# Two score rounds and two AV rounds at a time, gate steps spread over later pairs, and x rows stored unnormalised per pair

## The chip, the cores and the metric

The kernel runs on one core of a Trainium2 chip. The metric is the device time of one execution in microseconds (us). Instruction times come from one profiled execution; in its rows PE is TensorE's matmul side, PEld its weight loads, DVE is VectorE, ACT is ScalarE, POOL is GpSimd and SP the engine that issues most of the DMAs.

## The reference, cut to what matters

An attention with normalised q and k feeds a mixture of experts. The attention output, laid out as N = 3584 rows of 768 values, is the experts' input x; each row goes to the one expert with the highest logit, and each expert keeps at most 80 rows, those with the largest gate weight.

```python
# B, H, S, D = 8, 12, 448, 64;  E, F, capacity = 8, 1024, 80
q_n, k_n = rmsnorm(q, g_q), rmsnorm(k, g_k)
scores = scale * np.matmul(q_n, k_n.transpose(0, 1, 3, 2))
attn = np.exp(scores - np.max(scores, axis=-1, keepdims=True))
attn = attn / (np.sum(attn, axis=-1, keepdims=True) + 1e-09)
x = np.matmul(attn, v).transpose(0, 2, 1, 3).reshape(B * S, H * D)
logits = x @ w_gate
expert_idx = np.argmax(logits, axis=1)
gate_w = softmax(logits)[np.arange(N), expert_idx]
for e in range(E):
    tok_idx = the 80 (or fewer) rows of expert e with the largest gate_w
    h = np.maximum(x[tok_idx] @ w1[e], 0.0)
    out[tok_idx] = gate_w[tok_idx, None] * (h @ w2[e])     # all other rows stay 0
```

## The kernel before, in words

**Attention.** The 96 heads are worked off as 48 pairs; the loop variable is n, and six pairs make one batch b. A pair's 448 keys are cut into four groups of 112, j = 0 to 3. For each j, `score` makes two matmuls (one head on array rows 0 to 63, the other on 64 to 127) into one of two PSUM buffers `ps` of two banks each, and ACT takes the exponential into `at` (buffers for two pairs). `av` then makes two matmuls per j (one head on array columns 0 to 63, the other on 64 to 127) that add up in `po`. There is one `po` buffer: `uevac` copies it to SBUF (`us`) on DVE, and only then can the next pair's first `av` start. The softmax is left unnormalised; `presum` adds the four groups of `at` on DVE into `sm`, and `zl` turns the sums and `us` of two pairs into row sums and gate logits by narrow matmuls.

**Preparing q and k.** `load_qk` runs four pairs ahead into three buffers. `square` (ACT) and `rstd` (a DVE reduction into `ssq`, then `ms` and `rs` on POOL) run three pairs ahead, `normalise` (two DVE multiplications into `qn`) two ahead, and `transp` (PE transposes into a `tp` buffer of PSUM, copied out by ACT) one ahead. The two `tp` buffers are shared with the transposes of the gate and of x.

**Gate and x.** After a batch, `gate1` and `gate2` make the logits' normalisation, the maximum, the gate weight and the masked scores (DVE with one exponential on ACT and transposes on PE) and write them to `S_sb`. `xout` transposes `us` back, DVE multiplies by the reciprocal row sums `rz` into a bf16 row buffer `xb`, and one DMA per batch stores it to a DRAM scratch. `us` has 12 buffers for this.

**Order.** Inside the attention the order of every engine is that of the code (a manual schedule). Engines run their own instructions in that order, so an instruction that waits holds up all that stand behind it on its engine. SP issues loads, zero stores to `out` and the x stores in one queue in the same way.

**Top 80 and experts.** Ten rounds of maximum, index and replacement over `S_sb` (8 x 3584) run on DVE alone. Expert weights (24 KB per partition for w1 and w2 of one expert) are fetched by POOL's DMA queue: experts 0 and 1 during the attention, at n = 2, 5, 8 and 11 (`NW0 = 2`); the others have five slots in the space that the attention leaves, so ten transfers are queued when it is over, and expert 7 waits for a slot. Behind them on the same queue stand the gathers of the experts' rows (`xg`), which PE transposes (`pxt`) for the two matmul stages `ph` and `py`.

Of the kernel before, what the change touches and what calls it, by code (L numbers as in the profile page):

```python
# [19 lines left out]
def kernel(  # L20
# [31 lines left out]
    xbf_dram = nc.dram_tensor("xbf_scratch", (N, DM), BF16, kind="Internal").ap()  # L52
# [38 lines left out]
    NW0 = 2  # L91
# [20 lines left out]
    with tc.tile_pool(name="qk", bufs=3) as qkpool, \  # L112
# [3 lines left out]
         tc.tile_pool(name="us", bufs=12) as upool, \  # L116
# [118 lines left out]
        def gate1(b):  # L235
            zsb = gpool.tile([128, S], F32, tag="zsb", name="zsb", bufs=1)
            nc.vector.tensor_copy(zsb[:, :], gst[b]["zl"][:, :S])
            zt = tpps.tile([128, 512], F32, tag="tp", name="zt")
            for j in range(NT):
                nc.tensor.transpose(zt[:ST, j * 128:(j + 1) * 128],  # L240
                                    zsb[:, j * ST:(j + 1) * ST], ident[:, :])
            ztv = zt[:ST, :].rearrange("p (j c r) -> p j r c", j=NT, c=4)
# [11 lines left out]
            gst[b]["xb"] = gpool.tile([ST, NT, DM], BF16, tag="xb", name="xb")  # L254

        def gate2(b):
# [16 lines left out]
            nc.vector.tensor_mul(sc[:], eq[:], gw[:].unsqueeze(2).to_broadcast([ST, NT, E]))  # L273
            sp = tpps.tile([128, 512], F32, tag="tp", name="sp")
# [26 lines left out]
        for n in range(-4, NP + 6):  # L301
# [11 lines left out]
            m = n - 3  # L313
            if ok(n):
                score(n, 0)
            if ok(n - 2):
                uevac(n - 2)
            if ok(n - 1):
                av(n - 1, 0)
                presum(n - 1)  # L320
            if ok(n + 1):
                transp(n + 1, 0)
            if ok(n):
                score(n, 1)
            if ok(n - 1):
                av(n - 1, 1)
            if ok(n - 2) and (n - 2) % 2 == 1:
                zl(n - 2)
            if ok(n + 2):
                normalise(n + 2)  # L330
            if ok(n):
                score(n, 2)
            if ok(n - 1):
                av(n - 1, 2)
            if ok(n + 1):
                transp(n + 1, 1)
            if ok(n):
                score(n, 3)
            if ok(n + 3):
                square(n + 3)  # L340
                rstd(n + 3)
            if ok(n - 1):
                av(n - 1, 3)
# [32 lines left out]
    with tc.tile_pool(name="moe_w2", bufs=1) as wlate, \  # L376
# [6 lines left out]
        for e in range(E):  # L383
# [6 lines left out]
            xg = mpool.tile([CAP, DM], BF16, tag="xg", name="xg")  # L390
            nc.vector.memset(xg[:, :], 0.0)
            nc.gpsimd.indirect_dma_start(
                out=xg[:, :], out_offset=None, in_=xbf_dram[:, :],
                in_offset=bass.IndirectOffsetOnAxis(ap=idx_e[:, :1], axis=0),
                bounds_check=N - 1, oob_is_err=False)
            pxt = mps.tile([128, DC, CAP], BF16, tag="pxt", name="pxt")
# [69 lines left out]
```

## Time and profile before

| | us |
|---|---|
| median of 3 runs | 963.59 (961.34 to 969.52) |
| the profiled execution, its own time | 962.24 |
| its span, first to last instruction | 960.3 |
| PE busy in the span | 594.2 (62%) |
| DVE busy | 488.1 (51%) |
| ACT busy | 287.2 (30%) |
| POOL busy | 180.9 (19%) |

The span has four stages, one after the other: the attention, the top-80 rounds on DVE alone, a stretch in which only weight transfers run, and the experts. A busy share over the whole span therefore says little; each stage is read for itself. The granted clock stands beside the stages: 1.00 is 2.4 GHz and 0.50 is 1.2 GHz.

### The profile page before, as it was taken

How to read it: one execution, taken by the hardware profiler on the slowest of the kernel's cores; microseconds unless marked ns; L12 is line 12 of the kernel's file. 1: busy time of each engine (PE TensorE's matmuls, PEld its weight loads, DVE VectorE, ACT ScalarE, POOL GpSimd, SP SyncE). 2: the span in 40 equal slices, each digit the busy share in tenths (PEclk: the TensorE clock that was granted, in tenths of full speed). 3: DMA queues.
4: the chain of work that ended last, by engine and by line, in shares of the span. 5: the costliest groups of instructions: out<-in, count | busy, mean ns of one | idle time of the engine just before them, and what ended most of it. 6: DMA issues, size and time to landing. Idle time of an engine off the chain costs nothing.

```text
span 960.3 us, 7959 instructions
## 1 busy us (share of the span) xinstructions
PE 594.2 (62%) x3120; PEld 220.9 (23%) x3120; DVE 488.1 (51%) x589; ACT 287.2 (30%) x361; POOL 180.9 (19%) x134
## 2 busy tenths in 40 slices
PE   1888788868878887788888879879600000000746
PEld 0322222223222322322232223223200000000634
DVE  2655546545545544644644554564699997000212
ACT  2544433433443444344344334434000000000101
POOL 2422212221221221212221221220000001200212
PEclk9999988988898898799798888979855555555879
DMA  3456252521321222132023213101100001999371
GB/s 97 127 136 140 80 131 63 135 75 45 103 75 53 69 85 74 45 103 75 29 63 115 75 45 103 55 26 46 48 30 0 0 0 19 202 211 211 71 147 52
DMA packets 57893, 78.20 MB, mean 81 GB/s; under 512 B 6145, under 2 KB 46593, under 8 KB 57857
## 3 DMA queue, kind: packets, MB, share of 16 engines
q1 hardware_dynamic: 42368, 49.59, 17.2%
q0 software_dynamic: 15488, 28.12, 15.8%
q8 instruction: 24, 0.39, 0.2%
q14 instruction: 13, 0.10, 0.0%
HBM read 84.38 MB, written 18.49 MB: 107 GB/s over the span
## 4 chain that ended last, share of the span: by engine, by line
PE 48%; another core or an unknown queue 21%; DVE 11%; issue 7%; DMA 6%; ACT 4%; SPq 1%; POOL 1%; POOLq 0%; ACTq 0%; DVEq 0%
PE ps L189 18%; PE po L199 15%; PE tp L174 5%; DVE ssq L151 4%; ACT sq L145 4%; DMA out_dram<-yo,idx_e 3%; PE xp L285 3%; DMA vt<-in_v_dram 3%; PE zl L228 2%; PE zl L232 2%; DVE us L216 1%; DVE qn L165 1%; PE ph L409 1%; DVE S_sb L277 1%
## 5 line engine op out<-in xcount | busy, mean ns | idle before, releaser
L199 PE MATMUL po<-at,vt 112*64 112x448 f32 x768 | 205.8, 618 | 64.8 <-DVE us L216 35.0
L193 ACT ACTIVATE at<-ps 112x896 f32<-112x896 f32 x192 | 176.1, 917 | 231.8 <-PE ps L189 231.8
L189 PE MATMUL ps<-qkT 64*112 64x448 f32 x768 | 224.4, 666 | 0.6 <-ACT qkT L181 0.6
L151 DVE TENSOR_REDUCE ssq<-sq 112x16 f32<-112x1024 f32 x48 | 58.5, 1220 | 278.7 <-ACT sq L145 278.7
L157 POOL TENSOR_TENSOR rs<-ms,nhalf 112x16 f32<-112x16 f32 x48 | 140.1, 2918 | 4.0
L398 PE MATMUL pxt<-identb,xg 80*128 80x80 bf16 x48 | 3.5, 224 | 211.0 <-DMA xg<-xbf_scratch,idx_e 211.0
L154 POOL TENSOR_SCALAR ms<-ssq 112x16 f32<-112x16 f32 x48 | 10.6, 220 | 483.1 <-DVE ssq L151 483.1
L199 PEld LDWEIGHTS po<-at,vt 112*64 112x64 f32 x768 | 41.9, 146 | 216.8 <-issue 144.8
L413 ACT ACTIVATE h_sb<-ph 128x320 bf16<-128x320 f32 x16 | 7.0, 438 | 258.3 <-PE ph L409 258.3
L174 PE MATMUL tp<-ident,qn 112*128 112x112 f32 x384 | 65.8, 301 | 20.8 <-DVE qn L165 20.8
L189 PEld LDWEIGHTS ps<-qkT 64*112 64x112 f32 x768 | 59.4, 192 | 77.8 <-issue 48.0
L165 DVE TENSOR_TENSOR qn<-qk,rs 112x512 f32<-112x512 f32 x96 | 61.8, 685 | 11.7 <-POOL rs L157 11.7
L174 PEld LDWEIGHTS tp<-ident,qn 112*128 112x128 f32 x384 | 43.1, 156 | 97.3 <-issue 77.4
L179 ACT ACTIVATE qkT<-tp,gqk 128x448 f32<-128x448 f32 x48 | 30.5, 635 | 111.7 <-PE tp L174 111.7
L211 DVE TENSOR_TENSOR sm<-t,t 112x896 f32<-112x896 f32 x48 | 52.4, 1092 | 1.7
L209 DVE TENSOR_TENSOR t<-at 112x896 f32<-112x896 f32 x48 | 52.2, 1087 | 0.0
L210 DVE TENSOR_TENSOR t<-at 112x896 f32<-112x896 f32 x48 | 51.9, 1082 | 0.0
L398 PEld LDWEIGHTS <-xg 80*128 80x128 bf16 x48 | 2.8, 112 | 212.1 <-issue 197.9
L145 ACT ACTIVATE sq<-qk 112x1024 f32<-112x1024 f32 x48 | 50.4, 1049 | 1.3 <-DVE ssq L151 1.3
L401 DVE COPY xgT<-pxt 128x480 bf16<-128x480 bf16 x8 | 3.1, 393 | 92.3 <-PE pxt L398 92.3
L102 POOL DMA_DIRECT2D w_sb<-in_moe_w_dram x8 | 7.2, 897 | 175.2 <-DMA gw_scratch<-gw_all 168.9
L289 DVE TENSOR_TENSOR xb<-xp,rz 112x512 bf16<-112x512 f32 x48 | 31.7, 686 | 16.8 <-PE xp L285 16.5
(56 smaller groups left out, 458.7 us busy)
## 6 DMA issues: line engine op xcount, KB each, us to landing
w_sb<-in_moe_w_dram POOLq DMA_DIRECT2D x16, 1536.0 KB, 25.0
qk<-in_q_dram SPq DMA_DIRECT2D x48, 224.0 KB, 3.0
qk<-in_k_dram SPq DMA_DIRECT2D x48, 224.0 KB, 3.5
vt<-in_v_dram SPq DMA_DIRECT2D x48, 224.0 KB, 3.9
out_dram<-zeros SPq DMA_DIRECT2D x28, 384.0 KB, 4.5
xbf_scratch<-xb SPq DMA_DIRECT2D x8, 672.0 KB, 4.7
idx_e<-idx_scratch SPq DMA_DIRECT2D x8, 0.3 KB, 2.1
gw_e<-gw_scratch SPq DMA_DIRECT2D x8, 0.3 KB, 5.7
```

The source lines that it names most:

```text
L145: nc.scalar.activation(sq[:, :], st[n]["qk"][:].rearrange("p a h x -> p (a h x)"), AF.Square)
L151: nc.vector.reduce_sum(out=ssq[:, :], in_=st[n]["sq"][:].rearrange("p (g d) -> p g d", d=D), axis=AX.X)
L157: nc.gpsimd.tensor_tensor(rs[:].rearrange("p a h j -> p (a h j)"), ms[:, :], nhalf[:, :], op=ALU.pow)
L165: nc.vector.tensor_mul(qn[:, a].rearrange("p j h d -> p h j d"), qk[:, a].rearrange("p h (j d) -> p h j d", d=D), rs[:, a].unsqueeze(3).to ...
L174: nc.tensor.transpose(tp[:, j * ST:(j + 1) * ST], st[n]["qn"][:, a, j].rearrange("p h d -> p (h d)"), ident[:ST, :ST])
L189: nc.tensor.matmul(ps[:, hh, :S], st[n]["T1"][hh * D:(hh + 1) * D, j * ST:(j + 1) * ST], st[n]["T0"][hh * D:(hh + 1) * D, :], start=True, ...
L193: nc.scalar.activation(st[n]["at"][:, j], ps[:, :, :S], AF.Exp)
L199: nc.tensor.matmul(st[n]["po"][hh * D:(hh + 1) * D, :S], st[n]["v"][:, hh, j * D:(j + 1) * D], st[n]["at"][:, j, hh, :], start=(j == 0), s ...
L209: nc.vector.tensor_add(t0[:], at[:, 0], at[:, 1])
L210: nc.vector.tensor_add(t1[:], at[:, 2], at[:, 3])
L211: nc.vector.tensor_add(sm[:], t0[:], t1[:])
L289: nc.vector.tensor_mul(xb[:, :, hp * 128:(hp + 1) * 128].rearrange("p j (h d) -> p j h d", d=D), xp[:ST, :].rearrange("p (j h d) -> p j h ...
```

## The change

In the attention's loop body, the four score rounds and the four AV rounds of a pair are issued as two and two. The copy of `po` moves from the next pair's second step to the end of its own pair's AV rounds. `square` moves ahead of the transposes, `rstd` behind the last two score rounds. The gate of a batch is split into `gate1`, `gate1t`, `gate1v`, `gate2` and `gate3`, spread over three pairs. `xout` runs for one pair in every step, two pairs behind; its PSUM result is copied by ACT as f32 without the multiplication, and one DMA per pair stores it into a scratch whose rows hold 768 values and 12 reciprocal row sums; these are stored by one small DMA per batch. The experts gather such rows as f32 and multiply by the reciprocals on DVE into `xn`. `us` has 4 buffers instead of 12, three experts' weights are fetched during the attention instead of two, and the late slots are four instead of five; `xg`, `xgT` and `h_sb` have two buffers instead of three.

```diff
-    xbf_dram = nc.dram_tensor("xbf_scratch", (N, DM), BF16, kind="Internal").ap()
+    XW = DM + H
+    xr_dram = nc.dram_tensor("xr_scratch", (N, XW), F32, kind="Internal").ap()
...
-    NW0 = 2
+    NW0 = 3
...
-        slot = e if e < NW0 else NW0 + (e - NW0) % 5
+        slot = e if e < NW0 else NW0 + (e - NW0) % 4
...
-         tc.tile_pool(name="us", bufs=12) as upool, \
+         tc.tile_pool(name="us", bufs=4) as upool, \
...
+            nc.sync.dma_start(
+                out=xr_dram[b * S:(b + 1) * S, DM:XW].rearrange("(p j) h -> p j h", j=NT),
+                in_=rz[:].rearrange("p j i c -> p j (i c)"))
...
-            xb, rz = gst[b]["xb"], gst[b]["rz"]
-            r = rz[:].rearrange("p j i c -> p j (i c)")[:, :, 2 * hp:2 * hp + 2]
-            nc.vector.tensor_mul(
-                xb[:, :, hp * 128:(hp + 1) * 128].rearrange("p j (h d) -> p j h d", d=D),
-                xp[:ST, :].rearrange("p (j h d) -> p j h d", j=NT, d=D),
-                r.unsqueeze(3).to_broadcast([ST, NT, 2, D]))
-            if hp == HP - 1:
-                nc.sync.dma_start(
-                    out=xbf_dram[b * S:(b + 1) * S].rearrange("(p j) d -> p (j d)", j=NT),
-                    in_=xb[:].rearrange("p j d -> p (j d)"))
+            xb = prep.tile([ST, NT, 128], F32, tag="xb", name="xb")
+            nc.scalar.copy(xb[:].rearrange("p j d -> p (j d)"), xp[:ST, :])
+            nc.sync.dma_start(
+                out=xr_dram[b * S:(b + 1) * S, hp * 128:(hp + 1) * 128].rearrange(
+                    "(p j) d -> p j d", j=NT),
+                in_=xb[:])
...
             if ok(n):
                 score(n, 0)
-            if ok(n - 2):
-                uevac(n - 2)
+                score(n, 1)
+            for b in range(B):
+                last = b * HP + HP - 1
+                if n == last + 3:
+                    gate1(b)
+                if n == last + 4:
+                    gate1v(b)
             if ok(n - 1):
                 av(n - 1, 0)
+                av(n - 1, 1)
                 presum(n - 1)
+            if ok(n + 3):
+                square(n + 3)
             if ok(n + 1):
                 transp(n + 1, 0)
+                transp(n + 1, 1)
+            if ok(n + 2):
+                normalise(n + 2)
+            for b in range(B):
+                if n == b * HP + HP - 1 + 4:
+                    gate2(b)
             if ok(n):
-                score(n, 1)
+                score(n, 2)
+                score(n, 3)
+            if ok(n + 3):
+                rstd(n + 3)
             if ok(n - 1):
-                av(n - 1, 1)
+                av(n - 1, 2)
+                av(n - 1, 3)
+                uevac(n - 1)
+            if ok(n - 2):
+                xout(n - 2)
             if ok(n - 2) and (n - 2) % 2 == 1:
                 zl(n - 2)
...
             for b in range(B):
                 last = b * HP + HP - 1
-                if n == last + 2:
-                    gate1(b)
                 if n == last + 3:
-                    gate2(b)
-                if last + 3 <= n < last + 6:
-                    xout(b * HP + 2 * (n - last - 3))
-                    xout(b * HP + 2 * (n - last - 3) + 1)
+                    gate1t(b)
+                if n == last + 5:
+                    gate3(b)
...
-            xg = mpool.tile([CAP, DM], BF16, tag="xg", name="xg")
+            xg = mpool.tile([CAP, XW], F32, tag="xg", name="xg", bufs=2)
...
+            xn = mpool.tile([CAP, DM], BF16, tag="xn", name="xn", bufs=2)
+            nc.vector.tensor_mul(
+                xn[:].rearrange("p (h d) -> p h d", d=D),
+                xg[:, :DM].rearrange("p (h d) -> p h d", d=D),
+                xg[:, DM:XW].unsqueeze(2).to_broadcast([CAP, H, D]))
```

PE, one pair in the first batch, before: `ps` is a score round, `po` an AV round of the pair before it, `tp` the transposes for the pair after it; numbers behind a name are buffers as the program counts them.

```order
L189 MATMUL ps_584<-qkT_531,qkT_561 112x448 x2
L199 MATMUL po_590<-at_510,vt_369 64x448 x2
L174 MATMUL tp_599<-ident_58,qn_547 128x112 x4
L189 MATMUL ps_606<-qkT_531,qkT_561 112x448 x2
L199 MATMUL po_590<-at_510,vt_369 64x448 x2
L189 MATMUL ps_615<-qkT_531,qkT_561 112x448 x2
L199 MATMUL po_590<-at_510,vt_369 64x448 x2
L174 MATMUL tp_621<-ident_58,qn_547 128x112 x4
```

PE, one pair in the first batch, after; `xp` is the transpose of x, two pairs behind.

```order
L191 MATMUL ps_692<-qkT_646,qkT_653 112x448 x2
L191 MATMUL ps_696<-qkT_646,qkT_653 112x448 x2
L201 MATMUL po_700<-at_619,vt_462 64x448 x4
L176 MATMUL tp_713<-ident_58,qn_655 128x112 x4
L176 MATMUL tp_720<-ident_58,qn_655 128x112 x4
L191 MATMUL ps_730<-qkT_646,qkT_653 112x448 x2
L191 MATMUL ps_734<-qkT_646,qkT_653 112x448 x2
L201 MATMUL po_700<-at_619,vt_462 64x448 x4
L301 MATMUL xp_750<-ident_58,us_676 112x128 x4
```

Score and AV rounds that alternated one by one now stand in twos, both transposes stand together, and each pair has one group of `xp`.

ACT, one pair, before (`qkT` are the copies of the transposes, `sq` the square).

```order
L193 ACTIVATE at<-ps 112x896
L179 ACTIVATE qkT<-tp,gqk 128x448
L193 ACTIVATE at<-ps 112x896 x2
L181 COPY qkT<-tp 128x448
L193 ACTIVATE at<-ps 112x896
L145 ACTIVATE sq<-qk 112x1024
```

ACT, one pair, after.

```order
L195 ACTIVATE at_691<-ps_692 112x896
L195 ACTIVATE at_691<-ps_696 112x896
L147 ACTIVATE sq_711<-qk_613 112x1024
L181 ACTIVATE qkT_718<-tp_713,gqk_70 128x448
L183 COPY qkT_725<-tp_720 128x448
L195 ACTIVATE at_691<-ps_730 112x896
L195 ACTIVATE at_691<-ps_734 112x896
L304 COPY xb_755<-xp_750 112x512
```

The square now has the copies of the transposes and two exponentials behind it, and the copy of x has come onto ACT.

POOL's DMA queue behind the attention, from the last late weight transfers to the gathers, before: ten transfers (five experts, the last two of them shown) stand ahead of the first gather `xg`.

```order
L102 DMA w1_sb_4088<-in_moe_w1_dram 128x6x1024
L106 DMA w2_sb_4089<-in_moe_w2_dram 128x8x768
L102 DMA w1_sb_4092<-in_moe_w1_dram 128x6x1024
L106 DMA w2_sb_4093<-in_moe_w2_dram 128x8x768
L392 DMA xg_4104<-xbf_scratch,idx_e_4100 80x768
```

The same queue, after: all eight.

```order
L104 DMA w1_sb_4168<-in_moe_w1_dram 128x6x1024
L108 DMA w2_sb_4169<-in_moe_w2_dram 128x8x768
L104 DMA w1_sb_4172<-in_moe_w1_dram 128x6x1024
L108 DMA w2_sb_4173<-in_moe_w2_dram 128x8x768
L104 DMA w1_sb_4176<-in_moe_w1_dram 128x6x1024
L108 DMA w2_sb_4177<-in_moe_w2_dram 128x8x768
L104 DMA w1_sb_4180<-in_moe_w1_dram 128x6x1024
L108 DMA w2_sb_4181<-in_moe_w2_dram 128x8x768
L406 DMA xg_4192<-xr_scratch,idx_e_4188 80x780
```

Two transfers fewer stand ahead of the first gather.

## Rows read from the trace of the kernel before

**Rows 1.** Stretches: busy PE, PEld, DVE, ACT, POOL; then PEclk, DMA share, GB/s.

```profile
26.00:690.00 664.00, 542.58 (x2527) 181.66 (x2528) 347.81 (x485) 273.77 (x338) 148.07 (x96) 0.88 0.29 80
...
710.00:830.00 120.00, 0.00 (x0) 0.00 (x0) 99.71 (x48) 0.00 (x0) 7.71 (x9) 0.50 0.16 26
```

**Rows 2.** Timeline of PE, two pairs: start, length, instructions, idle time before and releaser.

```profile
42.02 0.97 PE L199 MATMUL po<-at,vt 112*64 112x448 f32 x4 [1.91 <-DVE us L216]
...
43.55 1.84 PE L189 MATMUL ps<-qkT 64*112 64x448 f32 x4
45.31 1.65 PE L199 MATMUL po<-at,vt 112*64 112x448 f32 x4
...
54.02 0.97 PE L199 MATMUL po<-at,vt 112*64 112x448 f32 x4 [1.91 <-DVE us L216]
54.93 0.60 PE L174 MATMUL tp<-ident,qn 112*128 112x112 f32 x4
55.46 1.01 PE L189 MATMUL ps<-qkT 64*112 64x448 f32 x4
56.40 0.97 PE L199 MATMUL po<-at,vt 112*64 112x448 f32 x4
57.30 0.96 PE L228 MATMUL zl<-sm,zsel 112*32 112x448 f32 x8
...
58.94 1.01 PE L189 MATMUL ps<-qkT 64*112 64x448 f32 x4
```

**Rows 3.** Timeline of DVE at the end of the second pair.

```profile
64.27 1.22 DVE L151 TENSOR_REDUCE ssq<-sq 112x16 f32<-112x1024 f32 x1 [5.95 <-ACT sq L145]
65.41 0.61 DVE L216 COPY us<-po 128x448 f32<-128x448 f32 x1
```

**Rows 4.** Busy time in two short stretches of the same two pairs.

```profile
43.50:46.80 3.30, 3.30 (x9) 0.74 (x8) 2.77 (x4) 1.55 (x2) 2.25 (x2) 0.51 0.55 159
...
54.00:64.00 10.00, 9.98 (x56) 3.09 (x56) 4.28 (x5) 4.63 (x6) 2.74 (x1) 1.00 0.65 185
```

**Rows 5.** Timeline of PE at the last pair, where four AV rounds stand together.

```profile
677.60 3.23 PE L199 MATMUL po<-at,vt 112*64 112x448 f32 x16 [0.73 <-DVE us L216]
680.75 0.96 PE L228 MATMUL zl<-sm,zsel 112*32 112x448 f32 x8
```

**Rows 6.** Groups by line and shape: busy us, mean ns, idle before and releaser.

```profile
L193 ACT ACTIVATE at<-ps 112x896 f32<-112x896 f32 x192 | 176.1, 917 | 231.8 <-PE ps L189 231.8
L157 POOL TENSOR_TENSOR rs<-ms,nhalf 112x16 f32<-112x16 f32 x48 | 140.1, 2918 | 4.0
L165 DVE TENSOR_TENSOR qn<-qk,rs 112x512 f32<-112x512 f32 x96 | 61.8, 685 | 11.7 <-POOL rs L157 11.7
L209 DVE TENSOR_TENSOR t<-at 112x896 f32<-112x896 f32 x48 | 52.2, 1087 | 0.0
L145 ACT ACTIVATE sq<-qk 112x1024 f32<-112x1024 f32 x48 | 50.4, 1049 | 1.3 <-DVE ssq L151 1.3
L289 DVE TENSOR_TENSOR xb<-xp,rz 112x512 bf16<-112x512 f32 x48 | 31.7, 686 | 16.8 <-PE xp L285 16.5
L179 ACT ACTIVATE qkT<-tp,gqk 128x448 f32<-128x448 f32 x48 | 30.5, 635 | 111.7 <-PE tp L174 111.7
```

**Rows 7.** Timeline of DVE from the last gate scores to the first top-80 round.

```profile
688.39 0.94 DVE L277 COPY S_sb<-sp 8x448 f32<-8x448 f32 x1 [1.00 <-PE sp L276]
...
694.25 3.87 DVE L362 MAX8 gw_all<-S_sb 8x8 f32<-8x3584 f32 x1
```

**Rows 8.** Timeline of POOL and PE: first late transfer, third gather's issue, first expert's transposes.

```profile
811.61 0.89 POOL L102 DMA_DIRECT2D w_sb<-in_moe_w_dram  x1 [168.89 <-DMA gw_scratch<-gw_all]
...
853.99 0.96 POOL L392 DMA_INDIRECT xg<-xbf_scratch,idx_e  x1 [6.42 <-issue]
...
891.31 0.96 PE L398 MATMUL pxt<-identb,xg 80*128 80x80 bf16 x12 [197.70 <-DMA xg<-xbf_scratch,idx_e]
```

**Rows 9.** The loads of q and k, issue to landing over all 96.

```profile
DMA to landing us min/median/max: 2.4/3.3/9.4
```

More of the change, by code (lines that the diff above doesn't have):

```diff
@@ L237, in gate1, with gate1t @@
             nc.vector.tensor_copy(zsb[:, :], gst[b]["zl"][:, :S])
+            gst[b]["zsb"] = zsb
+        def gate1t(b):
+            zsb = gst[b]["zsb"]
             zt = tpps.tile([128, 512], F32, tag="tp", name="zt")
@@ L241, in gate1, with gate1v @@
                                     zsb[:, j * ST:(j + 1) * ST], ident[:, :])
+            gst[b]["zt"] = zt
+        def gate1v(b):
+            zt = gst[b]["zt"]
             ztv = zt[:ST, :].rearrange("p (j c r) -> p j r c", j=NT, c=4)
@@ L273, in gate2, with gate3 @@
             nc.vector.tensor_mul(sc[:], eq[:], gw[:].unsqueeze(2).to_broadcast([ST, NT, E]))
+            gst[b]["sc"] = sc
+        def gate3(b):
+            sc = gst[b]["sc"]
             sp = tpps.tile([128, 512], F32, tag="tp", name="sp")
@@ L312 @@
                 fetch_w2(n // 6)
-            m = n - 3
             if ok(n):
                 score(n, 0)
-            if ok(n - 2):
-                uevac(n - 2)
+                score(n, 1)
[5 more added lines that the diff above has]
+                    gate1v(b)
             if ok(n - 1):
                 av(n - 1, 0)
+                av(n - 1, 1)
                 presum(n - 1)
+            if ok(n + 3):
+                square(n + 3)
             if ok(n + 1):
                 transp(n + 1, 0)
+                transp(n + 1, 1)
[4 more added lines that the diff above has]
+                    gate2(b)
             if ok(n):
-                score(n, 1)
+                score(n, 2)
+                score(n, 3)
+            if ok(n + 3):
+                rstd(n + 3)
             if ok(n - 1):
-                av(n - 1, 1)
+                av(n - 1, 2)
[3 more added lines that the diff above has]
+                xout(n - 2)
             if ok(n - 2) and (n - 2) % 2 == 1:
                 zl(n - 2)
[L329 to L343, printed above, removed]
             for b in range(B):
                 last = b * HP + HP - 1
-                if n == last + 2:
-                    gate1(b)
                 if n == last + 3:
-                    gate2(b)
-                if last + 3 <= n < last + 6:
-                    xout(b * HP + 2 * (n - last - 3))
-                    xout(b * HP + 2 * (n - last - 3) + 1)
+                    gate1t(b)
+                if n == last + 5:
+                    gate3(b)
         for i in range((NP + 6 + 1) // 2, N // 128):
@@ L388 @@
             nc.sync.dma_start(out=gw_e[:, :], in_=gw_dram[e, :, None])
-            xg = mpool.tile([CAP, DM], BF16, tag="xg", name="xg")
+            xg = mpool.tile([CAP, XW], F32, tag="xg", name="xg", bufs=2)
             nc.vector.memset(xg[:, :], 0.0)
             nc.gpsimd.indirect_dma_start(
-                out=xg[:, :], out_offset=None, in_=xbf_dram[:, :],
+                out=xg[:, :], out_offset=None, in_=xr_dram[:, :],
                 in_offset=bass.IndirectOffsetOnAxis(ap=idx_e[:, :1], axis=0),
                 bounds_check=N - 1, oob_is_err=False)
+            xn = mpool.tile([CAP, DM], BF16, tag="xn", name="xn", bufs=2)
[3 more added lines that the diff above has]
+                xg[:, DM:XW].unsqueeze(2).to_broadcast([CAP, H, D]))
             pxt = mps.tile([128, DC, CAP], BF16, tag="pxt", name="pxt")
             for c in range(DC):
-                nc.tensor.transpose(pxt[:, c, :], xg[:, c * 128:(c + 1) * 128],
+                nc.tensor.transpose(pxt[:, c, :], xn[:, c * 128:(c + 1) * 128],
                                     identb[:CAP, :CAP])
-            xgT = mpool.tile([128, DC, CAP], BF16, tag="xgT", name="xgT")
+            xgT = mpool.tile([128, DC, CAP], BF16, tag="xgT", name="xgT", bufs=2)
             nc.vector.tensor_copy(xgT[:], pxt[:])
-            h_sb = mpool.tile([128, FC, CAP], BF16, tag="hsb", name="h_sb")
+            h_sb = mpool.tile([128, FC, CAP], BF16, tag="hsb", name="h_sb", bufs=2)
             for fh in range(2):
```

1 line of the change is left out of this document (removed).

## The prediction

> **What bounds the kernel now.** I read the stages first [rows 1]. In the attention (26 to 690 us) PE is busy 543 of 664 us at a mean clock of 0.88, DVE 348; from 710 to 830 only DVE works, on the top-80 rounds, which the change does not touch. So I looked at the attention as PE's, and asked what ends PE's idle time.
>
> The timeline of two neighbouring pairs [rows 2] shows it. Both pairs begin with PE idle for 1.91 us, released by DVE's copy `us`. PE's next AV round needs the one `po` buffer, and the copy that frees it stands on DVE behind the reduction `ssq`, which waited 5.95 us for ACT's `sq` [rows 3]; `sq` is the last thing that ACT does in a pair. So the wait is made by the order of the code: square, reduction, copy, next AV round, one after the other, with PE standing still. Plain pairs take 12.0 us (42.02 to 54.02). From the first pair shown to the last, 42.02 to 677.60 [rows 2, 5], there are 46 pairs in 635.6 us, 13.82 each: the gate and x steps add 1.8 us per pair on the mean, since they put more DVE work ahead of the same copy.
>
> Behind the pause the clock falls in some pairs: from 43.5 to 46.8 us it is 0.51, 1.2 GHz, and in the next pair 1.00 over ten us [rows 4]. A score round that takes 0.94 us at 1.00 (55.46 to 56.40) took 1.76 there, and the AV round behind it 1.65 instead of 0.90 [rows 2]. That is 1.5 us in one of these two pairs, 0.75 per pair.
>
> The last stretch hangs on the weight queue [rows 8]: the first late transfer is issued at 811.61, the first expert's transposes start at 891.31, as soon as the first gather has landed behind ten transfers. At 853.99 the third gather is issued because the fifth transfer has landed, so the last five took 37.3 us, 7.46 each.
>
> **The attention after the change, part by part.** *The pause.* The copy of `po` is now issued at the end of its own pair. Between the last AV round and the next one that needs `po`, PE has the transposes of x, in every second pair `zl`, and two score rounds: 0.53 + 1.69 us at the least, and the copy takes 0.61 [rows 3]. The reduction ahead of it on DVE needs `sq`, which ACT now makes behind its second exponential. Does DVE get through? Its load per pair is three additions of 1.09, two multiplications of 0.69, one reduction of 1.22 and one copy of 0.61, 6.5 us [rows 3, 6]. What is late next is then PE itself. I cost the pause at nothing left; if that cover failed, it would cost up to the 1.9 us per pair that it costs today.
>
> *PE's work per pair at clock 1.00.* The four AV rounds that stand together take 3.15 us, 677.60 to 680.75 [rows 5]; alone, a round takes 0.905 (54.02 to 54.93). Four times the round plus one switch is 3.15, the round plus one switch is 0.905: a round is 0.75, the switch 0.16. So two AV rounds take 1.65 us, and two score rounds, alone 0.94, by the same step 1.69. Two groups of `tp` take 0.53 each (54.93 to 55.46), 1.06. One group of `xp` per pair I take as another 0.53 (four transposes as well). `zl` takes 1.64 (57.30 to 58.94) every second pair, 0.82. The two gate transposes are two groups of 0.53 in six pairs, 0.18. Sum: 3.38 + 3.30 + 1.06 + 0.53 + 0.82 + 0.18 = 9.27 us.
>
> *Does anything else take longer than 9.27?* I walk one pair with PE's start at 0. The first score round ends at 0.94, its exponential (0.92) at about 1.9 and the second at 2.8; PE needs these two PSUM buffers again only at 1.69 + 1.65 + 1.06 = 4.4. `sq` (1.05) runs to 3.9, the copies of the transposes (0.64 at most each) to 5.2. The third score round ends at 5.35, its exponential and the fourth's at 7.2; the next pair's first round comes at 8.27, or 9.9 with `zl`. The copy of x starts at 8.3 and ends at 8.9. ACT's sum is four times 0.92, 1.05, two of 0.64 and one of about 0.6 (the 448-column copies scaled to 512), 6.6 us. The reduction on DVE runs at about 4 to 5.2, POOL's power of 2.92 [rows 6] ends near 8.5, and `normalise` asks for it in the next pair behind 3.3 us of additions. In the pair that carries `gate2` the exponentials three and four come some 2 us later, until 9.3, but that pair has `zl`, and PE asks at 9.9 and 10.75. No wait of PE is left in this walk.
>
> *Where the x multiplication goes.* 0.69 us per pair leaves DVE [rows 6] and a copy of about 0.6 us comes to ACT; neither is on the path, given the walk. SP gets 48 stores of 512-byte rows, eight of the reciprocals and two more fetches beside them. Each store waits for the copy of x at 8.9 us, and the loads of q and k for a later pair stand behind it in SP's queue. They are issued by about 10.2 us, land 3.3 us later (at most 9.4 so far), and `square` asks for them two pairs on, at 2 x 9.27 + 2.9 = 21.4. I cost it at nothing; the price without that cover is the third rival [rows 9].
>
> *Sum for the attention:* 46 pairs by 13.82 - 9.27 = 4.55 us, 209 us. Of the 4.55, 1.9 is the pause, 0.75 the clock, 0.7 the switches saved by twos, and about 1.1 what the gate and x steps add today beyond PE's own work. The start (first 40 us, waits for loads and POOL) I leave as it is, within 2 us either way.
>
> *End of the attention.* The last gate copy ends at 689.33 and the first top-80 round starts at 694.25, behind the last x multiplications on DVE [rows 7]: 4.9 us that go, less about 1 us for a group of transposes that now stands ahead of the last `zl`. Take 4.
>
> **Weights and experts.** Eight transfers instead of ten stand ahead of the first gather: 2 x 7.46 = 14.9 us, or 15.9 by the mean of all ten (79.7 us, [rows 8]). I take 15. Expert 7's weights now wait for the fourth slot's expert 3 instead of the third's 2, one expert later, and one expert more is computed before that stall, so the rest of the stage keeps its length. The third prefetch runs beside the attention like the other two; the first of those is issued at n = 2, and that pair (42.02 to 54.02) took 12.0 us, as the plain pairs do [rows 2]. Added: rows of 3,120 bytes instead of 1,536, 250 KB a gather, at the weights' pace (1,536 KB in 7.46 us) 0.6 us more; the multiplication into `xn`, 768 columns at 0.69 us per 512, 1.0 us, open at the first expert and once behind the stall. Take 2 us more for the stage, bounds 0 and 8 (one each for eight experts).
>
> **Sum.** 962.2 - 209 - 4 - 15 + 2 = 736 us, against the profiled execution's own 962.24; the median of the runs shown is 1.4 us above that, which I do not carry.
>
> **The rivals.** *The slow stretches stay (second most likely).* The same pause of 1.91 us stands ahead of both pairs [rows 2], yet only one of them ran at 0.51 [rows 4]; so the rows show that the fall comes behind the pause, not that the pause is enough for it. If something else makes it, 0.75 us per pair stays, or 1.5 if it then takes every pair: 736 + 35 to 736 + 69, 771 to 805. For it: transposes of three kinds now stand together in the loop. Against it: ten us of close work at 1.00. The Trainium skill's page "TensorE: Matmul & The Clock Gate", section "Why this matters for your kernels", ties a fall to idle gaps of TensorE longer than the one seen here; by that rule the pause would not be the cause and this rival's time would stand. The trace does not bear it out, since the fall follows pauses of 1.91 us.
>
> *A new wait inside the pair.* Two score rounds now need both PSUM buffers free at once, and `square` has ACT's copies and two exponentials behind it. If the walk misses 0.5 to 1 us per pair of hand-overs, the pair is 9.8 to 10.3 us and the time 759 to 783. Against it: the tightest step of the walk has 1 us to spare.
>
> *Slower: loads late for `square`.* One mechanism: SP's store waits for the copy of x at the pair's end, the loads of q and k behind it slip, `square` waits for them at ACT's head, and the transposes' copies and the exponentials behind it hold PE. It begins when loads take 21.4 - 10.2 = 11.2 us to land, and each further us costs 46 us. The gain of 226 us is gone at 4.9 us beyond, so from 16 us in every pair the kernel is slower than before, at 18 us by 46 x 1.9 = 87 us: 1050. Against it: no load took over 9.4 us, with a median of 3.3 [rows 9]; for it, shorter pairs and row-wise stores ask more of the DMA queues.
>
> **How the numbers follow.** Forecast 80% (with its own bounds of 720 to 757: PE's pair at 9.0 to 9.6 us, start and experts as above), slow stretches 11%, new wait 7%, late loads 2%. The likeliest gives 736. From 720 to 785 lie the forecast, the new wait and the lower part of the slow stretches, about 9 in 10; a narrower end would cut into the forecast's own bounds. A measurement here tells 1% from no change, some 9 us, the width of the runs shown. All cases but the last are faster by far more: faster 0.97; same 0.01 for a late-load case that happens to balance; slower 0.02.
>
> **What would show it.** Right: PE's idle time released by `us` in single us; a clock of 0.97 or more through the attention; pairs 9.1 to 9.6 us apart; the first top-80 round near 481 us; the first transposes of the experts some 182 us behind it instead of 197. Wrong: stretches near 0.5 inside the pairs, exponentials that PE waits for, `sq` idle on loads of q and k, or first transposes no earlier behind the top-80 rounds.

## The result and the profile after

| | us |
|---|---|
| median after, 4 runs | 670.38 (670.23 to 671.67) |
| median before, beside it | 963.58 |
| ratio | 0.696 (0.693 to 0.699) |
| the profiled execution after, its own time | 670.38 |
| its span | 668.2 |

The kernel became 293 us faster; forecast were 226 us. 670 us lies 50 us under the low end of the range.

The granted clock and the busy time in four stretches of the changed kernel, in the columns of [rows 1] (after the length: busy PE, PEld, DVE, ACT, POOL, then PEclk, DMA share, GB/s):

```profile
42.00:150.00 108.00, 108.00 (x629) 43.93 (x629) 77.89 (x100) 71.29 (x97) 42.53 (x30) 1.00 0.76 179
150.00:300.00 150.00, 150.00 (x878) 61.91 (x876) 113.19 (x157) 99.35 (x136) 51.67 (x35) 1.00 0.57 147
300.00:450.00 150.00, 150.00 (x876) 61.66 (x872) 107.81 (x152) 96.57 (x133) 45.53 (x29) 1.00 0.38 110
470.00:590.00 120.00, 0.00 (x0) 0.00 (x0) 116.44 (x54) 0.00 (x0) 3.83 (x5) 0.50 0.58 105
```

In the attention PE now works without a gap at 2.4 GHz: 408 of 408 us, where [rows 1] had 543 of 664 at 0.88. The fourth row matters as much. It is the stage of the top-80 rounds, DVE alone as before, but DMA share 0.58 where [rows 1] has 0.16: transfers run under the rounds.

PE's timeline from one pair into the next, which answers to [rows 2]:

```profile
147.20 1.76 PE L191 MATMUL ps<-qkT 64*112 64x448 f32 x8
148.89 1.72 PE L201 MATMUL po<-at,vt 112*64 112x448 f32 x8
150.55 0.99 PE L176 MATMUL tp<-ident,qn 112*128 112x112 f32 x8
151.46 1.76 PE L191 MATMUL ps<-qkT 64*112 64x448 f32 x8
153.15 1.72 PE L201 MATMUL po<-at,vt 112*64 112x448 f32 x8
154.81 0.65 PE L301 MATMUL xp<-ident,us 128*112 128x128 f32 x4
155.29 0.60 PE L246 MATMUL zt<-ident,zsb 128*112 128x128 f32 x4
155.82 1.76 PE L191 MATMUL ps<-qkT 64*112 64x448 f32 x8
```

No row has a bracket, so nothing is waited for. From start to start, two score rounds take 1.69 us, two AV rounds 1.66, the transposes 0.91 and `xp` 0.58 (144.98 to 145.56 in the pair ahead, not shown). The one wait for the copy of `po` left in the whole attention, 0.7 us, is for the copy of the first pair's, the 39.97 row below. The last row below, 457.50, answers to [rows 5]:

```profile
39.97 1.72 PE L201 MATMUL po<-at,vt 112*64 112x448 f32 x8 [0.71 <-DVE us L218]
...
457.50 3.23 PE L201 MATMUL po<-at,vt 112*64 112x448 f32 x16
```

46 pairs lie between the same two AV rounds, 417.5 us, 9.08 each. Over this whole stretch, before and after (columns as above):

```profile
42.02:677.60 635.58, 520.54 (x2421) 173.16 (x2421) 329.62 (x456) 262.39 (x323) 139.97 (x91) 0.88 0.29 80
39.97:457.50 417.53, 417.53 (x2432) 170.79 (x2432) 305.64 (x415) 272.14 (x369) 141.76 (x93) 1.00 0.54 140
```

So of the 218 us, 115 were PE's idle time and 103 are a shorter busy time for the same work. Before, PE's longest single waits in the attention were on the gate's steps (us in total, times, longest):

```profile
PE sp L276 <- DVE sc L273: 34.5, 8, 4.4
...
PE zt L240 <- DVE zsb L237: 20.6, 8, 2.8
```

About 51 of the 115 us are such waits on the gate (the last batch's 4 us lie behind the stretch), nearly all the rest are waits ahead of `po`. The end of the attention and the start of the top-80 rounds on DVE, as in [rows 7]:

```profile
469.88 0.93 DVE L293 COPY S_sb<-sp 8x448 f32<-8x448 f32 x1 [1.09 <-PE sp L292]
470.84 3.88 DVE L376 MAX8 gw_all<-S_sb 8x8 f32<-8x3584 f32 x1
```

POOL's first and last late weight transfer and its first gather, which answer to [rows 8]:

```profile
466.95 0.89 POOL L104 DMA_DIRECT2D w_sb<-in_moe_w_dram  x1 [35.88 <-DVE lx L258]
...
472.88 0.95 POOL L108 DMA_DIRECT2D w_sb<-in_moe_w_dram  x1
590.71 1.06 POOL L406 DMA_INDIRECT xg<-xr_scratch,idx_e  x1 [116.88 <-DMA gw_e<-gw_scratch]
```

The first late transfer is not released by `gw_scratch<-gw_all`, the store behind the last top-80 round, as in [rows 8], but by a gate step of the last batch (`lx`), 4 us ahead of the first round. All eight are issued by 474 us and run while DVE works; from 540 to 590 us, with the rounds still running, nothing is transferred any more (DMA share 0.00):

```profile
540.00:590.00 50.00, 0.00 (x0) 0.00 (x0) 47.06 (x24) 0.00 (x0) 0.00 (x0) 0.50 0.00 0
```

The first gather waits for a load of the rounds' result (`gw_e`), not for a transfer. PE's first transposes of the experts, and the one long wait left among them:

```profile
595.47 0.56 PE L417 MATMUL pxt<-identb,xn 80*128 80x80 bf16 x6 [125.63 <-DVE xn L411]
...
641.38 0.58 PE L417 MATMUL pxt<-identb,xn 80*128 80x80 bf16 x6 [11.69 <-DVE xn L411]
```

Where the time went, from these rows and [rows 2, 5, 7, 8]:

| | before | after | moved | forecast |
|---|---|---|---|---|
| start, to the first AV shown | 42.02 | 39.97 | -2.0 | 0 |
| first AV to last | 635.6 | 417.5 | -218.1 | -209 |
| last AV to first top-80 round | 16.65 | 13.34 | -3.3 | -4 |
| first round to first `pxt` | 197.1 | 124.6 | -72.4 | -15 |
| first `pxt` to the end of the span | 69.0 | 72.7 | +3.7 | +2 |

With 0.2 us more outside the span that is the whole 291.9 between the profiled executions. The miss of 66 us is 57 us in the fourth line and 9 in the second.

### The profile page after: what moved, and what is told of

Its sections match the earlier page's. It is cut to its first block, busy times and chain, and to the rows that moved or that the text cites. A ratio compares the mean times of both kernels' runs of the same rounds, so it can differ in the third digit from the quotient of the medians.

```text
span 668.2 us, 8151 instructions
## 1 busy us (share of the span) xinstructions
PE 487.4 (73%) x3120; PEld 216.7 (32%) x3120; DVE 467.7 (70%) x549; ACT 298.2 (45%) x409; POOL 182.4 (27%) x134
## 5 line engine op out<-in xcount | busy, mean ns | idle before, releaser
L195 ACT ACTIVATE at<-ps 112x896 f32<-112x896 f32 x192 | 165.7, 915 | 72.0 <-PE ps L191 66.8
L191 PE MATMUL ps<-qkT 64*112 64x448 f32 x768 | 170.7, 563 | 3.0 <-ACT qkT L183 2.0
L201 PE MATMUL po<-at,vt 112*64 112x448 f32 x768 | 165.3, 552 | 0.7 <-DVE us L218 0.7
L218 DVE COPY us<-po 128x448 f32<-128x448 f32 x48 | 29.9, 623 | 81.0 <-PE po L201 81.0
L201 PEld LDWEIGHTS po<-at,vt 112*64 112x64 f32 x768 | 46.7, 136 | 109.1 <-issue 88.3
L176 PE MATMUL tp<-ident,qn 112*128 112x112 f32 x384 | 48.3, 269 | 19.0 <-DVE qn L167 19.0
L176 PEld LDWEIGHTS tp<-ident,qn 112*128 112x128 f32 x384 | 38.1, 143 | 52.7 <-issue 23.9
L304 ACT COPY xb<-xp 112x512 f32<-112x512 f32 x48 | 28.2, 588 | 52.2 <-PE xp L301 49.6
L406 POOL DMA_INDIRECT xg<-xr_scratch,idx_e x8 | 8.7, 1087 | 130.1 <-DMA gw_e<-gw_scratch 116.9
L376 DVE MAX8 gw_all<-S_sb 8x8 f32<-8x3584 f32 x10 | 38.8, 3882 | 0.3
```

The lines of the kernel that those rows point to most:

```text
L176: nc.tensor.transpose(tp[:, j * ST:(j + 1) * ST], st[n]["qn"][:, a, j].rearrange("p h d -> p (h d)"), ident[:ST, :ST])
L191: nc.tensor.matmul(ps[:, hh, :S], st[n]["T1"][hh * D:(hh + 1) * D, j * ST:(j + 1) * ST], st[n]["T0"][hh * D:(hh + 1) * D, :], start=True, ...
L195: nc.scalar.activation(st[n]["at"][:, j], ps[:, :, :S], AF.Exp)
L201: nc.tensor.matmul(st[n]["po"][hh * D:(hh + 1) * D, :S], st[n]["v"][:, hh, j * D:(j + 1) * D], st[n]["at"][:, j, hh, :], start=(j == 0), s ...
L376: nc.vector.max(out=mv, in_=S_sb[:, :])
```

## The experiments

My theory after the result: the late weight slots no longer share addresses with tiles that live through the top-80 rounds, so the wait of [rows 8] is gone; the attention is as forecast. The rival for the weights: the transfers are merely shorter or fewer, or the third prefetch matters. For the attention the parts of the forecast's 4.55 us per pair were undone by themselves, all but the moved x multiplication, which no run put back.

**e1: the gate pool first.** The changed kernel, with the pool that holds the tiles of the top-80 rounds put at the front of the attention's pools, so that it lies where the late slots will lie. Nothing else moves.

```diff
-    with tc.tile_pool(name="qk", bufs=3) as qkpool, \
+    with tc.tile_pool(name="gate", bufs=2) as gpool, \
+         tc.tile_pool(name="qk", bufs=3) as qkpool, \
...
-         tc.tile_pool(name="gate", bufs=2) as gpool, \
```

> The changed kernel with the gate's tile pool placed first in SBUF instead of last among the attention's pools, so that the late weight slots lie over the gate's tiles; four late slots and three early experts stay. Theory 'place': the late transfers of the changed kernel start under the top-80 rounds only because their four slots (96 KB) end below the gate's tiles, the last to be released; here they must wait for the store of the top-80 gate weights again, issue about 118 us later (near 588 us instead of 467) and eight transfers of 7.46 us stand ahead of the first gather: 670 + 58 = 728 us, 715 to 735. Rival 'count': the transfers start early because there are eight instead of ten, or because of the third early expert: no change, 670 us.

Measured: 730.97 us, ratio 0.758 (0.755 to 0.760), against 0.696. POOL's first late transfer, and PE's first transposes:

```profile
588.78 0.89 POOL L104 DMA_DIRECT2D w_sb<-in_moe_w_dram  x1 [157.76 <-DMA gw_scratch<-gw_all]
```

```profile
654.93 0.56 PE L417 MATMUL pxt<-identb,xn 80*128 80x80 bf16 x6 [184.56 <-DVE xn L411]
```

The wait of [rows 8] is back by place alone, with as many transfers of the same size, and costs 60.6 us. The rivals fall. The first top-80 round starts at 471.38 us here, so the first transposes come 183.6 us behind it: with the wait in place, the 182 that the prediction named is nearly met.

**e2: four late slots in the kernel before.** The mirror: the five late slots take 120 KB per partition, four take 96.

```diff
-        slot = e if e < NW0 else NW0 + (e - NW0) % 5
+        slot = e if e < NW0 else NW0 + (e - NW0) % 4
```

> The kernel before with one edit: four late weight slots instead of five. Theory 'place': 96 KB end below the gate's tiles (which start at about 108 KB there, and five slots take 120), so eight of twelve late transfers run under the top-80 rounds: the first gather lands some 75 us earlier; experts 6 and 7 both wait for a slot now, two transfers more behind the third and fourth experts, 15 us back. 963.6 - 75 + 15 = 903 us, 890 to 915. Rival 'loop': the early start needs the changed attention loop (the x rows leave the gate's pool there): the transfers still start at 811 us and the time is 963 to 980.

Measured: 904.36 us, 0.940 (0.935 to 0.944), 59.5 us off the kernel before by one digit. POOL's first late transfer, and the stall that fewer slots cost PE later:

```profile
693.51 0.89 POOL L102 DMA_DIRECT2D w_sb<-in_moe_w_dram  x1 [51.51 <-PE xp L285]
```

```profile
816.45 0.56 PE L398 MATMUL pxt<-identb,xg 80*128 80x80 bf16 x6 [123.56 <-DMA xg<-xbf_scratch,idx_e]
...
867.76 0.58 PE L398 MATMUL pxt<-identb,xg 80*128 80x80 bf16 x6 [27.86 <-DMA xg<-xbf_scratch,idx_e]
```

The first transposes come 75 us earlier than in [rows 8]; some of that is given back at 867.76, where two experts now wait for a slot.

**e3: single rounds.** The changed kernel with score and AV rounds alternating one by one again, the rest of the body in its new order.

```diff
             if ok(n):
                 score(n, 0)
-                score(n, 1)
...
             if ok(n - 1):
                 av(n - 1, 0)
+            if ok(n):
+                score(n, 1)
+            if ok(n - 1):
                 av(n - 1, 1)
...
                 score(n, 2)
+            if ok(n - 1):
+                av(n - 1, 2)
+            if ok(n):
                 score(n, 3)
...
             if ok(n - 1):
-                av(n - 1, 2)
                 av(n - 1, 3)
```

> The changed kernel with score and AV rounds issued one by one again (score, AV, score, AV, transposes, score, AV, score, AV); all else as in the changed kernel, the copy of po at the pair's end, square and gate places too. Theory 'switch': a round that follows one of the other kind costs 0.16 (AV) or 0.19 (score) us more than one that follows its own kind, so the pair gets 2 x 0.16 + 2 x 0.19 = 0.69 us longer, 48 pairs: 670 + 33 = 703 us, at a clock of 1.00. Rival 'no switch cost': the pair keeps 9.08 us and the time 670; the gain of the attention is pause, clock and gate alone.

Measured: 702.77 us, 0.729 (0.727 to 0.732). PE has no gap here either:

```profile
42.00:450.00 408.00, 408.00 (x2216) 141.33 (x2218) 280.55 (x376) 255.54 (x341) 136.58 (x91) 1.00 0.54 137
```

The kernel takes 32.4 us longer. 31.9 of them lie between the two AV rounds of the table (39.98 and 489.40 us here), 0.69 per pair, the price worked out in the prediction from [rows 2, 5].

**e4: the square early in the kernel before.** One line moved, nothing else: ACT squares before the pair's later exponentials, so DVE's reduction no longer holds up the copy of `po`.

```diff
             if ok(n):
                 score(n, 1)
+            if ok(n + 3):
+                square(n + 3)
...
-                square(n + 3)
```

> The kernel before with one line moved: square is issued behind the second score round instead of behind the fourth; the DVE order is the same. Theory 'square': the pause of 1.91 us at the start of each pair comes from the chain square, reduction, copy; in plain pairs it goes, the clock stays at 1.00 there and a plain pair takes 9.3 to 9.7 instead of 12.0 us; pairs that carry gate or x steps (four of six) keep a part of their waits, since these steps stand ahead of the copy on DVE. About 1.7 to 2.7 us per pair over 46 pairs: 963.6 less 80 to 125, 840 to 885 us. Rival 'one po buffer': the copy itself is too late wherever the square stands, the pause stays: 955 to 965.

Measured: 808.57 us, 0.839 (0.836 to 0.842), 155 us off, more than expected. The stretch between the same two AV rounds as in the table:

```profile
40.27:524.41 484.14, 455.46 (x2422) 154.53 (x2420) 331.32 (x456) 262.26 (x324) 139.42 (x91) 1.00 0.38 105
```

and PE's waits over the whole span (us in total, times, longest):

```profile
PE po L199 <- PE ps L189: 15.0, 21, 1.0
PE sp L276 <- DVE sc L273: 9.8, 8, 3.6
...
PE po L199 <- DVE us L216: 3.4, 8, 0.7
```

The pauses on `us` and the stretches at half clock went together. Between these AV rounds 151 us are gone, and the two rows (this one and that of the kernel before, above) split them: PE is idle 28.7 us instead of 115.0, 1.9 less per pair, and busy 455.5 instead of 520.5 for the same work, 1.4 less per pair, at a clock of 1.00 instead of 0.88. The expectation had let the pairs with gate or x steps keep a part of their waits. DVE's order is the same here, but the gate's steps too stand behind the reduction, and come sooner with it: PE's waits for `sc` fall from 34.5 to 9.8 us, those for `zsb` from 20.6 to 0.7.

**e5: the square late in the changed kernel.** The opposite: `square` back behind the last score round, all else as after.

```diff
-            if ok(n + 3):
-                square(n + 3)
...
             if ok(n + 3):
+                square(n + 3)
                 rstd(n + 3)
```

> The changed kernel with square moved back behind the fourth score round; all else as changed. By the walk: the fourth exponential ends near 7.1 us of a pair, square then runs to 8.1, the reduction to 9.4, the copy of po to 10.0; PE asks for po behind two score rounds at 9.9 in a pair without zl and 11.5 with it. Theory 'cover': the two score rounds and the x transposes now cover the chain that made the pause before, so at most 0.3 us per second pair is lost: 670 to 680 us. Rival 'square alone': the place of square decides here as in the kernel before, some 155 us are lost: 800 us or more.

Measured: 677.95 us, 0.703. PE's waits:

```profile
PE po L201 <- DVE us L218: 7.0, 7, 1.6
```

Seven waits instead of one in 48 pairs. In the changed loop, with the copy at the end of its own pair, the place of the square matters little: 7.6 us here, 155 in e4.

**e6: the gate in one pair.** All gate steps at once in the new loop; the kernel before had them in two neighbouring pairs.

```diff
-                if n == last + 3:
-                    gate1(b)
-                if n == last + 4:
-                    gate1v(b)
...
-                if n == b * HP + HP - 1 + 4:
-                    gate2(b)
...
                 if n == last + 3:
+                    gate1(b)
                     gate1t(b)
-                if n == last + 5:
+                    gate1v(b)
+                    gate2(b)
                     gate3(b)
```

> The changed kernel with all gate steps of a batch (gate1, gate1t, gate1v, gate2, gate3) issued in one place, at the end of the third pair behind the batch, instead of over three pairs. Theory 'gate waits': PE waits there for the copy of zl (0.8 us) and for the chain from the gate's transposes to its scores (3.7 us, as at the very end of the changed kernel's attention), 4.5 us in each of seven batches, 31 us, up to 45 if the clock falls behind these pauses: 700 to 715. Rival 'no cost': the steps are hidden anyway: 670 to 673.

Measured: 715.75 us, 0.743 (45.4 us more, at the upper end of what was expected). PE's timeline of one gate, and the clock in that stretch:

```profile
163.37 0.62 PE L246 MATMUL zt<-ident,zsb 128*112 128x128 f32 x4 [0.77 <-DVE zsb L239]
167.65 0.91 PE L292 MATMUL sp<-ident,sc 112*8 112x112 f32 x4 [3.66 <-DVE sc L285]
168.49 3.33 PE L191 MATMUL ps<-qkT 64*112 64x448 f32 x8
171.75 1.87 PE L201 MATMUL po<-at,vt 112*64 112x448 f32 x8
```

```profile
168.40:171.70 3.30, 3.30 (x9) 1.08 (x8) 3.07 (x4) 0.92 (x1) 0.00 (x0) 0.50 0.68 211
172.00:184.00 12.00, 12.00 (x74) 4.78 (x73) 8.06 (x11) 7.77 (x10) 3.10 (x2) 1.00 0.28 68
```

PE waits 4.4 us for DVE's chain of small steps, and the score rounds behind the wait take 3.33 instead of 1.76 at a clock of 0.50: 6.0 us, and seven of the eight batches have their gate inside the loop, 42 us of the 45.

**e7: the copy of `po` late.** The changed kernel with the copy of a pair's `po` behind the next pair's additions and multiplications on DVE.

```diff
             if ok(n - 1):
+                presum(n - 1)
+            if ok(n + 2):
+                normalise(n + 2)
+            if ok(n - 2):
+                uevac(n - 2)
+            if ok(n - 1):
                 av(n - 1, 0)
                 av(n - 1, 1)
-                presum(n - 1)
...
-            if ok(n + 2):
-                normalise(n + 2)
...
-                uevac(n - 1)
```

> The changed kernel with the copy of po put behind presum and normalise of the next pair on DVE, which makes PE wait for it again: about 2.4 us at the start of a pair that follows one without zl, 0.8 us otherwise, 78 us over 48 pairs. Theory 'the pause brings the clock down': stretches at 1.2 GHz appear behind the longer pauses, as in the kernel before, and cost up to another 1.5 us in every second pair: 748 to 785, mean clock in the attention 0.95 or below. Rival 'not the pause': clock 1.00 throughout, 740 to 750.

Measured: 844.59 us, 0.876: the kind of loss was right, the size far off. PE over four pairs, and the clock in three stretches of them:

```profile
152.44 3.25 PE L201 MATMUL po<-at,vt 112*64 112x448 f32 x8 [4.17 <-issue]
...
165.58 1.72 PE L201 MATMUL po<-at,vt 112*64 112x448 f32 x8 [0.52 <-PE ps L191]
...
175.04 1.72 PE L201 MATMUL po<-at,vt 112*64 112x448 f32 x8 [1.21 <-DVE us L218]
...
188.91 3.25 PE L201 MATMUL po<-at,vt 112*64 112x448 f32 x8 [3.97 <-issue]
```

```profile
152.40:157.00 4.60, 4.56 (x16) 2.23 (x16) 2.07 (x2) 0.33 (x1) 3.35 (x2) 0.50 1.14 255
157.30:188.00 30.70, 25.91 (x149) 10.09 (x148) 15.93 (x19) 17.60 (x24) 8.04 (x6) 0.99 0.48 111
188.90:192.00 3.10, 3.09 (x8) 0.83 (x8) 1.04 (x1) 0.00 (x0) 1.88 (x2) 0.50 1.09 246
```

Six pairs from 152.44 take 78.3 us, 13.05 each: 16.0 us of pauses, and the rest beyond 9.08 is slow clock behind the three pauses of about 4 us. The 188.91 row names "issue", but it is the copy that PE needs. DVE's timeline of that pair shows what stands ahead of it:

```profile
183.32 0.63 DVE L239 COPY zsb<-zl 128x448 f32<-128x448 f32 x1 [6.27 <-PE zl L234]
183.86 1.08 DVE L211 TENSOR_TENSOR t<-at 112x896 f32<-112x896 f32 x1
...
188.20 0.62 DVE L218 COPY us<-po 128x448 f32<-128x448 f32 x1
```

The expectation had counted the work ahead of the copy, not that this work itself waits, here for `zl`.

**e8: two lines in the kernel before.** e2 and e4 together, both diffs as above.

> The kernel before with two one-line edits together: square behind the second score round, and four late weight slots instead of five. The two act in different stages (attention; top-80 rounds and experts), so the sum of the two single edits is expected: 963.85 - 155.3 - 59.5 = 749 us. Rival 'shared': one of the two takes away what the other gives (the eight transfers start earlier or later against the last loads): 765 or more.

Measured: 748.23 us, 0.775 (0.771 to 0.780). The two gains add up: 59.5 + 155.3 = 214.8 us expected, 216.6 measured against the kernel before beside it (964.85). Two one-line edits give 217 us, where the change gives 293.

**e9: the last weights early.** A version beyond the change. Expert 7's weights go into the slot of expert 0, which is free after the first expert, and the gathers of six experts are issued ahead of that fetch; for the space, `S_sb` moves into the gate pool, and the small index and weight tiles get a buffer per expert.

```diff
-        for e in range(NW0, E):
+        for e in range(NW0, E - 1):
...
+            if e == 1:
+                w1_sb = wpool.tile([128, DC, F], BF16, tag="w1_0", name="w1_sb")
+                w2_sb = wpool.tile([128, FC, DM], BF16, tag="w2_0", name="w2_sb")
+                w_tiles[E - 1] = (w1_sb, w2_sb)
+                fetch_w1(E - 1)
+                fetch_w2(E - 1)
...
-            xg = mpool.tile([CAP, XW], F32, tag="xg", name="xg", bufs=2)
+            xg = mpool.tile([CAP, XW], F32, tag="xg", name="xg", bufs=4)
```

> The changed kernel with expert 7's weights in the slot of expert 0 instead of expert 3, four gather buffers and eight index buffers instead of two and three (S_sb moves from the constants into the gate's pool to make room for them). The first six gathers then stand ahead of the last two weight transfers, which start behind the first expert instead of the fourth. Theory 'last stall': the changed kernel's experts stand still for 11.7 us until a gather has landed behind these two transfers, and some 3 us more in shorter waits for gathers; both go: 670 - 12 to 670 - 16, 654 to 658 us. Rival 'other end': the stage is bound by the chain gather, copy, matmuls, scatter of each expert, and the time moves to other waits: 664 to 672.

Measured: 651.43 us (650.63 to 653.64), 0.676 (0.673 to 0.678): 19 us under the changed kernel, faster than both theories had it. POOL's sixth gather and, right behind it, the fetch:

```profile
599.72 0.95 POOL L412 DMA_INDIRECT xg<-xr_scratch,idx_e  x1 [1.13 <-DVE xg L411]
600.67 0.92 POOL L103 DMA_DIRECT2D w_sb<-in_moe_w_dram  x1
```

In the changed kernel the same fetch is issued at 620 us and the next gathers queue behind it: that is the stall of 11.69 us at 641.38. Here no wait of PE among the experts exceeds 2.7 us, and its waits for gathered rows behind the first transposes, 14.9 us in the changed kernel, are gone; where the other 4 of the 19 us come from was not traced.

**e10: two early experts.** The changed kernel with one prefetch fewer.

```diff
-    NW0 = 3
+    NW0 = 2
```

> The changed kernel with two experts fetched during the attention instead of three (late slots four, as changed). Theory 'place': what the third prefetch gives is only the stall of the experts' stage, since eight transfers hide under the top-80 rounds either way; experts 6 and 7 both wait for a slot, two transfers of 7.5 us more: 670 + 15 = 685 us, as in the kernel before with four slots. My recorded prediction's step (two transfers fewer ahead of the first gather) would give the same 15 us, but ahead of the first gather; where the 15 us lie tells the two apart.

Measured: 686.36 us, 0.712 (0.709 to 0.715). PE's first transposes and the stall:

```profile
595.17 0.56 PE L417 MATMUL pxt<-identb,xn 80*128 80x80 bf16 x6 [125.64 <-DVE xn L411]
...
649.88 0.58 PE L417 MATMUL pxt<-identb,xn 80*128 80x80 bf16 x6 [27.84 <-DVE xn L411]
```

The third prefetch brings 16 us, all in the later stall, which is 16.2 us longer here; the first transposes start as in the changed kernel. Against what was expected of it, this run does not test the prediction's 15 us: four slots put eight transfers ahead of the first gather with or without the third prefetch. That the experts' stage keeps its length with the third prefetch, as the prediction said, it bears out.

## Why the prediction was wrong

**The step that failed is that on the weights:** "Eight transfers instead of ten stand ahead of the first gather", 15 us. It counted transfers and kept, unasked, the wait ahead of them. [rows 8] showed that wait in its own bracket, 168.89 us for `gw_scratch<-gw_all`, and I did not ask why a weight transfer should wait for the result of the top-80 rounds. The answer is place: the late slots lie in the space that the attention leaves, and 120 KB of them reached into the tiles of the rounds; 96 KB do not. Added up from the tile sizes in the code, the pools ahead of those tiles take some 108 KB per partition before and 98 KB after, since `us` has shrunk; by this sum five slots would reach into them either way, so it is the count of the slots that decides. e1 puts the overlap back (+60.6 us), e2 takes it out of the kernel before (-59.5). What was measured in place of 15 us is 72.4 from the first round to the first transposes. Some 13.5 of it stay in e1 (197.1 to 183.6): that is the forecast step, 15 less the 0.6 and 1.0 priced for the longer gather and `xn`. The other 59 are the wait that was kept. In the changed kernel the transfers cost nothing ahead of the first gather, since all of them end under the rounds (the 540 to 590 row), and the third prefetch pays only in the later stall.

**The attention** was right in mechanism and 9 us short. The pair takes 9.08 us, not 9.27. The term that was mis-sized is that of the transposes: 1.06 us taken for two groups of `tp`, 0.91 measured where they stand together, 0.15 of the 0.19. Part of the rest is the stretch itself: its last pair has no score rounds of a next one and the pair ahead of it no transposes, 2.6 us or 0.06 per pair. The other terms held: 1.69 and 1.66 for the rounds in twos (taken: 1.69 and 1.65), 0.58 for `xp` (taken: 0.53).

**Its parts.** *Switches:* 0.7 us per pair taken, 0.69 measured (e3). *Pause, gate and x:* 1.9 and about 1.1 taken, 3.0 together. The 1.9 was that of two pairs, not the mean: PE's 115 us of idle time are 2.5 per pair, about 1.4 ahead of `po` and 1.1 on the gate's own steps, which the prediction had read as DVE work ahead of the copy. All gate steps in one place of the new loop cost 45 us (e6). *Clock:* 0.75 taken from two pairs. Of the 103 us of shorter busy time 32 are the switches (e3) and 65 the clock as e4 has it, 1.4 per pair; the 6 left are about the 0.15 per pair of the transposes. The split was thus off on both sides; the forecast did not suffer, since it took the whole 13.82 less the new work. e4 shows that the order of the square made most of the pauses and the slow stretches in the kernel before, so the prediction's chain of square, reduction and copy holds. In the changed kernel the square's place hardly matters (e5). No run moved the copy alone in the kernel before, so what that move is worth by itself stays open. e7 puts the copy further back on DVE than the kernel before had it, so its 174 us are the price of that place, not what the copy's move brought.

**The rivals.** *The slow stretches stay:* they did not, the clock is 1.00 through the attention, with three kinds of transposes in the loop. The Trainium skill's page "TensorE: Matmul & The Clock Gate", section "Why this matters for your kernels", which this rival went by, warns only of idle gaps longer than the 1.91 us seen before the change. e6 and e7 agree with it, as the clock is 0.50 behind pauses of 3.66 and 3.97 us; the kernel before does not, since 1.91 us is the longest pause in the 20 us ahead of the fall at 43.5 us [rows 2, 4], and e4, without those pauses, has none. *A new wait inside the pair:* none, PE is busy 408 of 408 us. *Late loads:* loads of q and k landed within 13.1 us at most, more than the 9.4 of [rows 9] and, in the worst case, more than the 11.2 from which I let the rival begin; but the median was 4.0, and `square` waited 8.3 us in all, none of it passed on to PE:

```profile
L147 ACT ACTIVATE sq<-qk 112x1024 f32<-112x1024 f32 x48 | 50.7, 1057 | 14.3 <-DMA qk<-in_k_dram 8.3
```

**The rest.** End of the attention: 4 taken, 3.3 measured. Experts: +2 taken, +3.7 measured, within its bounds of 0 and 8. Start: 2 us earlier, at the edge of the 2 either way. Of the signs named, those on the attention came true (9.08 us per pair lies just under its 9.1); the first top-80 round came at 470.8 instead of 481, and the first transposes 125 us behind it instead of 182. The range failed because its low end, 720, held only the bounds of the attention, the start and the experts: no case in it let the weight transfers start earlier.

## What to carry to other kernels

When a row's bracket names a releaser that the work doesn't need by its data, ask for the buffer behind it: a pool that reuses space starts with whatever still lives at its addresses, and a smaller pool, or another order of pools, can start a transfer a whole stage earlier (60 us here). Price a change of a buffer count by what it releases, not only by how many transfers are left. And before rewriting a loop, try the one line that moves a late producer: moving the square alone gave 155 us in the kernel before, where the whole change gave 218 in the attention.

## What was not expected of the hardware

Where the clock fell and where not, by the rows: two AV rounds took 3.25 us behind pauses of 3.97 and 4.17 us, and 1.72 behind 0.52 and 1.21 (e7). In the kernel before, a pause of 1.91 us preceded both a pair with a slow stretch and one without [rows 2, 4]. What tells those two pairs apart stays open; no run tried it. Also not expected: eight transposes in a row take 0.91 us where two groups of four apart take 1.06 [rows 2], so a second group right behind the first costs 0.38.
